# Loops on VectorE and ScalarE, and a semaphore for each pair of engines, in a decode kernel of grouped-query attention beside a Mish block

## The chip, the core and the metric

The kernel runs on one core of a Trainium2 chip. Its engines work side by side: TensorE (matmuls; PE in the profile, and PEld for its weight loads), VectorE (DVE), ScalarE (ACT), GpSimd (POOL) and SyncE (SP), which here issues the big loads. Each has its own stream of instructions and takes them in order; between engines only semaphores order the work. The 16 DMA engines of the core bring data from memory into the on-chip memory, and also the engines' own instructions. The metric is the device time of one launch in microseconds (us), the median of several runs.

## The reference

Eight sequences decode one token each. Two branches read the same `x` (8 rows of 512) and are added to it:

```python
xn = _layernorm(x, axis=-1)
return x + _A_ref(xn, A_k_cache, A_v_cache, A_wq, A_wo) + _B_ref(xn, B_w1, B_b1, B_w2)
```

`_A_ref` is attention with 32 query heads on 8 key/value heads (4 queries each), over a cache of 8192 positions of 128 numbers: `q = xn @ wq`, scores against all keys, softmax, the weighted sum of the values, `@ wo`. `_B_ref` is a dense layer of 1792, the Mish activation `h * tanh(softplus(h))` and a dense layer back to 512. All is float32. The two caches alone are 537 MB, and each of their bytes is used once.

## The kernel before

**Packs.** The work on the caches is cut into 16 packs (`PACKS`). A pack is a pair of key/value heads of two sequences; for each of the two sequences, `b` = 0 and 1, it has 8 MB of keys and 8 MB of values. Pack `p` computes its own scores and weights and, in the same stretch, the output of pack `p - 1`, whose weights are ready. The main loop (line 916 on) does this for each `b`:

- `scores(b, ...)`: 32 matmuls of the pack's queries `qT[:, b]` with 16 blocks of keys, into `C[b]`; ScalarE copies the result to `sc`; `rows(b)` puts it in place in `S`.
- Between the two, on TensorE, the leftovers of the pack before: `sums`, `merge`, and on VectorE `over` (one over the softmax's sums) and `collect`; every fourth pack also `turn`, which brings four packs' outputs into the layout for `wo`.
- After `rows(1)`: `maximum` (VectorE and TensorE by turns), `expand(p + 1)` (VectorE writes the next pack's `qT`, one product for each `b`), `exponents` (ScalarE, then a transpose on VectorE), `fold`, `weights`, `row_sums`.
- `values(b, ...)`: 32 matmuls of the weights `pt` with the values, into `O[b]`; `gather(b)` on VectorE adds up the parts of `O[b]` into `os`.
- In some packs `queries` (a new pair of heads, with `wq`) or `outputs` (with `wo`).

**Loads.** There are three places for streamed data: `kva`, `kvb` and `kvw`. After pack 0 the keys go through `kvb`, which is a quarter larger than one load, so that a load may start when three quarters of the keys before it have been read (the blocks are read forwards and backwards by turns). The values go through `kva`, the projection weights through `kvw`. `plan` (line 357) queues the loads in a fixed order, `pump` and `release` (346 to 355) issue the next one when its place is free. All go out from SyncE in that order, one `dma_start` each, and wait on TensorE's semaphore for the last matmul that reads what they overwrite. So a load that waits holds up the loads behind it.

**The recording layer.** The kernel's calls are recorded by `Program` (line 69), which finds for each operation which earlier ones it must wait for, and `emit` (190) writes the instructions. Each engine counts up one semaphore. TensorE's packs 1 to 15 are one body in a loop on TensorE (`nc.tensor.Fori`, line 253), with tests for the parts that not every pack has. A body that is the same in each pass can't wait for a growing count, so what TensorE waits for is given as tokens (`token="dve"`, `"act"`, `"ev"`) which it takes back by lowering the semaphore (`take`, line 124). In `expand` the token is on the product of `b` = 1 (line 599), and TensorE takes it ahead of `scores` of `b` = 0 (line 923). VectorE, ScalarE, GpSimd and SyncE have all 16 packs written out, one after the other. Where a pack's buffers rotate, `ring` (324) gives two (`os`, `nms`, `l`, `ls`, `r`, `nr`). Line 228 is the one place in `issue` where instructions are made, so nearly all rows of the profile name it.

```python
with nc.tensor.Fori(*LOOP) as pack:
    for name, ops in body:
```

Of the kernel before, what the change touches and what calls it, by code (L numbers as in the profile page):

```python
# [12 lines left out]
P = 128  # L13
# [48 lines left out]
STREAMS = ("k0", "k1", "k", "v", "v0", "va", "vb", "w", "wa", "wb", "w1", "b1", "w2a", "w2b", "w2c")  # L62


ENGINES = ("vector", "scalar", "gpsimd", "sync", "tensor")
LOOP = (1, PACKS)


class Program:
# [4 lines left out]

    def __init__(self, nc):
        self.nc = nc
        self.ops = {e: [] for e in ENGINES}
        self.know = {e: {} for e in ENGINES}
        self.seen = {}
        self.given, self.taken = {}, {}  # L80
        self.signals = set()
        self.pack, self.parts = None, {}
        self.before, self.after = [], []
        self.on_chip, self.psum = set(), set()

    def __getattr__(self, engine):
        if engine not in ENGINES:
            raise AttributeError(engine)
        return Engine(self, engine)

# [6 lines left out]
    def learn(self, engine, op):  # L97
        know = self.know[engine]
        for who, n in (*op.clock.items(), (op.who, op.n)):
            know[who] = max(know.get(who, -1), n)  # L100

    def enter(self, pack):
        self.pack = pack
        if pack is not None:
            self.parts[pack] = []
            self.part(None)

    def part(self, name):

        if self.pack is not None:  # L110
            self.parts[self.pack].append((name, []))

    def keep(self, op):

        if self.pack is None:
            at = self.after if self.parts else self.before
            at.append(op)
            op.place = (self.parts != {}, len(at))
        else:
            parts = self.parts[self.pack]  # L120
            parts[-1][1].append(op)
            op.place = ("loop", len(parts), len(parts[-1][1]))

    def take(self, sem, n=1):

        self.taken[sem] = self.taken.get(sem, 0) + n
        op = Op("tensor", "take", (sem, n), {})
        op.who, op.n, op.waits = "tensor", -1, []
        self.learn("tensor", self.given[sem][self.taken[sem] - 1])
        self.keep(op)  # L130

    def add(self, op, outs, ins, token=None, stream=None):
        engine = op.engine
        op.who = stream or engine
        needs = []
        for ap, writes in [(a, False) for a in ins] + [(a, True) for a in outs]:
            r = self.region(ap)
            seen = self.seen.setdefault(ap.tensor.name, {})
            psum = ap.tensor.name in self.psum
            bank = (r[2] // 512, (r[3] - 1) // 512)  # L140
            for (who, wrote, q), o in seen.items():
                if who == "tensor" == engine:
                    continue
                both = r[0] < q[1] and q[0] < r[1] and r[2] < q[3] and q[2] < r[3]
                hit = both and (writes or wrote)
                if psum and who != engine:
                    hit = bank[0] <= (q[3] - 1) // 512 and q[2] // 512 <= bank[1]
                if hit and self.know[engine].get(who, -1) < o.n:
                    needs.append(o)
        op.waits = []  # L150
        for o in sorted(needs, key=lambda o: -len(o.clock)):
            if self.know[engine].get(o.who, -1) >= o.n:
                continue
            latest = max((x for x in needs if x.who == o.who), key=lambda x: x.n)
            if engine == "tensor" and latest.who in self.given and latest.who in STREAMS:
                self.take(latest.who, latest.n + 1 - self.taken.get(latest.who, 0))
                continue
            assert engine != "tensor" or self.pack is None, (op.method, op.args, latest.who)
            self.wait(op, latest)
        op.token = token  # L160
        if engine == "tensor":
            self.keep(op)
        everyone = self.given.setdefault(stream, []) if stream else self.ops[engine]
        op.n = len(everyone)
        op.clock = dict(self.know[engine])
        everyone.append(op)
        if stream:
            self.ops[engine].append(op)
        if token:
            self.given.setdefault(token, []).append(op)  # L170
        for ap, writes in [(a, False) for a in ins] + [(a, True) for a in outs]:
            self.seen[ap.tensor.name][op.who, writes, self.region(ap)] = op
        return op

    def wait(self, op, other):
        if other.who == "tensor":
            self.signals.add(other.place)
        elif other.token:
            rest = self.ops[other.who][other.n :]
            other = next(o for o in rest if not o.token and o.who == other.who)  # L180
        self.learn(op.engine, other)
        op.waits.append(other)

    def end(self, op):

        last = Op("sync", "done", (), {})
        last.who, last.n, last.waits = "sync", len(self.ops["sync"]), [op]
        self.ops["sync"].append(last)

    def emit(self, tests):  # L190
        nc = self.nc
        sems = {}

        def sem(name):
            if name not in sems:
                sems[name] = nc.alloc_semaphore(f"s_{name}")
            return sems[name]

        count = {}
        for e in ENGINES:  # L200
            n = 0
            for op in self.ops[e]:
                if op.who != e:
                    count[op] = 16 * (op.n + 1)
                elif (op.place in self.signals) if e == "tensor" else not op.token:
                    n += 1
                    count[op] = n

        def issue(op):
            engine = getattr(nc, op.engine)  # L210
            if op.method == "take":
                name, n = op.args
                n *= 16 if name in STREAMS else 1
                engine.wait_ge(sem(name), n).then_inc(sem(name), -n)  # L214
                return
            *first, last = op.waits or [None]
            for w in first:
                engine.wait_ge(sem(w.who), count[w])
            if op.method == "done":
# [9 lines left out]
            if last is not None:  # L229
                got.wait_op(sem(last.who), count[last], "sem-ge")  # L230
# [4 lines left out]
            elif op.engine != "tensor" or op.place in self.signals:  # L235
                got.then_inc(sem(op.engine), 1)
# [802 lines left out]
```

## Time and profile before

| | |
|---|---|
| median of 3 runs | 1309.33 us (1309.3 to 1311.3) |
| the profiled execution | 1311.0 us |
| its span, first to last instruction | 1308.8 us |
| TensorE busy | 881.2 us, 67% of the span |
| VectorE busy | 386.0 us, 592 instructions |
| ScalarE busy | 122.2 us, 294 instructions |
| read from memory | 561.01 MB, 429 GB/s over the span |
| mean granted clock of TensorE | 0.832 |

How to read it. The span is what the profiler saw between the first and the last instruction; the execution's own time is 2.2 us longer. A row of the timeline has the start in us, the duration, the engine, the line, the operation, what it writes and reads, and in brackets how long the engine had been idle before it and what ended that. SPq is SyncE's queue: the row of a load is its issue. The DMA view gives for each kind of load its count and the microseconds from issue to landing; issue plus that number is the landing. Its queue rows give packets, MB and the share of the 16 DMA engines' time in the stretch that was asked for; "instruction" marks an engine's own code. A row of the waits gives who waited for whom: us in total, how often, the longest.

### The profile page before, as it was taken

What the parts mean: (1) busy time and instruction counts of PE and PEld (TensorE: products, weight loads), DVE (VectorE), ACT (ScalarE), POOL (GpSimd) and SP (SyncE); (2) the same over time, 40 slices, a digit from 0 to 9 for tenths busy, and PEclk for the clock granted to TensorE, in tenths of its full rate; (3) what the DMA queues carried; (4) which work ended last, traced back from release to release, by engine and by line L of the source; (5) the groups of instructions that cost most, each with busy time, mean ns of one, the idle gap of its engine ahead of it and who ended that gap; (6) DMA issues with size and microseconds to landing.
All of it is one profiled execution on the core that took longest, in us unless ns stands there. A gap on an engine that the chain in (4) does not pass through costs nothing. (4 is left out here: it accounts for less than half of the span.)

```text
span 1308.8 us, 10954 instructions
## 1 busy us (share of the span) xinstructions
PE 881.2 (67%) x4766; PEld 321.2 (25%) x4766; DVE 386.0 (29%) x592; ACT 122.2 (9%) x294; POOL 4.8 (0%) x10
## 2 busy tenths in 40 slices
PE   5886657856568765686656686665775656766666
PEld 1222222322222222232222222222232222322223
DVE  6250504305051140521405032052320505114051
ACT  1020202001020100201102020020200102001020
POOL 1000000000000000000000000000000000000000
PEclk8887789887888777887877887778887878877779
DMA  9999999999999999999999999999999999999997
GB/s 402 445 415 435 427 447 421 443 425 441 425 443 423 443 423 441 424 443 425 439 431 437 411 449 427 429 439 427 441 427 439 429 437 431 433 429 435 423 434 325
DMA packets 11414, 561.25 MB, mean 429 GB/s; under 512 B 1276, under 2 KB 1408, under 8 KB 1544
## 3 DMA queue, kind: packets, MB, share of 16 engines
q1 hardware_dynamic: 11376, 561.06, 99.4%
q8 instruction: 6, 0.10, 0.0%
q14 instruction: 8, 0.07, 0.0%
q10 hardware_dynamic: 24, 0.02, 0.0%
HBM read 561.01 MB, written 0.07 MB: 429 GB/s over the span
## 5 line engine op out<-in xcount | busy, mean ns | idle before, releaser
L228 PE MATMUL c<-kvb,qT 128*64 128x512 f32 x1984 | 501.1, 669 | 325.9 <-PEq L214 325.9
L228 PEld LDWEIGHTS c<-kvb,qT 128*64 128x64 f32 x1984 | 170.2, 154 | 656.7 <-issue 656.7
L228 PE MATMUL o<-kva,pt 128*32 128x512 f32 x1984 | 249.9, 656 | 23.7 <-PEq L214 23.7
L228 DVE TENSOR_REDUCE nm<-s 128x1 f32<-128x1024 f32 x16 | 19.6, 1225 | 448.4 <-PE s L228 448.4
L228 PEld LDWEIGHTS o<-kva,pt 128*32 128x32 f32 x1984 | 95.6, 119 | 170.2 <-issue 154.8
L228 DVE STREAM_TRANSPOSE raw<-e 128x2048 f32<-128x2048 f32 x36 | 126.3, 3507 | 19.4 <-ACT e L228 18.8
L228 ACT COPY sc<-c 128x512 f32<-128x512 f32 x32 | 18.8, 586 | 981.0 <-PE c L228 981.0
L228 ACT ACTIVATE e<-s,nms 128x512 f32<-128x512 f32 x128 | 88.0, 688 | 133.3 <-DVE nms L228 69.8
L228 DVE RECIPROCAL r<-m 128x16 f32<-128x16 f32 x16 | 4.1, 257 | 234.9 <-PE m L228 234.9
L228 DVE TENSOR_SCALAR os<-o,isel 128x128 f32<-128x128 f32 x32 | 11.2, 351 | 153.4 <-PE o L228 153.4
L228 DVE TENSOR_TENSOR pt<-raw 64x256 f32<-64x256 f32 x128 | 53.6, 418 | 3.6
L228 PE MATMUL s<-sc,csel 64*128 64x512 f32 x128 | 37.9, 664 | 11.0 <-PEq L214 11.0
L228 DVE TENSOR_TENSOR raw<-raw 128x1024 f32<-128x1024 f32 x32 | 39.2, 1225 | 1.1
L228 DVE TENSOR_TENSOR qT<-qc,bsel 128x1024 f32<-128x1024 f32 x32 | 37.7, 1219 | 0.0
L228 DVE SCALAR_TENSOR_TENSOR os<-o,isel,os 128x128 f32<-128x128 f32 x96 | 33.7, 351 | 3.4
L228 ACT ACTIVATION_READ_ACCUMULATOR e<-s,nms 128x1 f32 x128 | 24.7, 193 | 0.0
L228 PE MATMUL m<-ident,nm 128*1 128x128 f32 x16 | 4.4, 276 | 22.6 <-PEq L214 22.6
L228 PE MATMUL h<-kvw,xnT 128*64 128x512 f32 x64 | 17.5, 696 | 0.0
L228 DVE TENSOR_SCALAR e<-h 128x512 f32<-128x512 f32 x16 | 11.1, 691 | 18.3 <-PE h L228 17.9
L228 PE MATMUL m<-hsel,os 128*128 128x8 f32 x66 | 12.5, 262 | 4.7 <-DVE os L228 3.3
L228 PEld LDWEIGHTS m<-hsel,os 128*128 128x128 f32 x66 | 9.9, 190 | 18.8 <-issue 12.2
L228 PEld LDWEIGHTS s<-sc,csel 64*128 64x128 f32 x128 | 10.8, 190 | 14.6 <-issue 14.4
(87 smaller groups left out, 163.0 us busy)
## 6 DMA issues: line engine op xcount, KB each, us to landing
kvw<-in_wq SPq DMA_DIRECT2D x4, 2048.0 KB, 30.5
kvw<-in_wo SPq DMA_DIRECT2D x3, 2048.0 KB, 29.9
kva<-in_v SPq DMA_DIRECT2D x1, 6144.0 KB, 25.0
kva<-in_w SPq DMA_DIRECT2D x1, 3584.0 KB, 15.8
kva<-in_v SPq DMA_DIRECT2D x1, 2048.0 KB, 28.1
kvb<-in_w SPq DMA_DIRECT2D x1, 2048.0 KB, 20.3
kvw<-in_wo SPq DMA_DIRECT2D x2, 1024.0 KB, 24.3
kvb<-in_w SPq DMA_DIRECT2D x1, 1024.0 KB, 24.1
```

What stands on the lines that cost most here:

```text
L228: got = getattr(engine, op.method)(*op.args, **op.kw)
```

## The change

The recording layer is written anew, and the kernel's order of calls is kept but for small shifts. What it does:

1. **Loops on three engines.** TensorE, VectorE and ScalarE each have packs 1 to 15 as one body in a loop of their own, with tests for `turn`, `queries` and `outputs` where the engine has a part in them. VectorE's written-out stream of packs becomes a prologue with pack 0, the body, and an end part; so does ScalarE's. GpSimd and SyncE stay written out.
2. **A semaphore for each pair.** An operation signals at most one engine, on a semaphore named after giver and receiver (`vector_tensor`, `tensor_sync`, ...); parts that are not in every pack have semaphores of their own. `giver` picks the operation whose signal covers a need: the one needed, or the first later one that signals the same receiver. At the end of each pass the receiver lowers its semaphores by what a pass adds. TensorE's `take` instructions inside the body go.
3. **Relays.** Where an operation already signals one engine and a second needs to know, the first receiver passes it on: a wait that signals. The load that overwrites values waits for such a relay on VectorE, placed ahead of `gather`; those of `wq`, `wo` and `w1` go through VectorE too, and the first load of values through ScalarE (ahead of its copy). Loads of keys still wait for TensorE directly.
4. **Register addresses.** `expand` and `collect` differ from pack to pack in where they read or write; in the body the address comes from the loop's register (`vary`).
5. **One buffer for each tile.** `ring` goes; `nms`, `l`, `ls`, `rt`, `nr` are single, `os` is one for each `b`. `collect` moves ahead of `over`, since `rt` is single. Two memsets are added to the prologue (`rt` and 16 columns of `M`), one goes.
6. **Signals of `expand`.** In pack 0 and in the body, the product of `b` = 0 signals TensorE; that of `b` = 1 signals nobody, and is covered by a later signal.
7. **The end.** GpSimd's clearing of the semaphores, beside the output's transfer, goes.

The core of it (left out: the bookkeeping that numbers the signals, and the renaming of tiles):

```diff
-LOOP = (1, PACKS)
+LOOPED = ("tensor", "vector", "scalar")
+FIRST, END = 1, PACKS
...
+    def relay(self, engine, to, after):
+        return self.add(Op(engine, "relay", to=to), [after])
...
-        for e in ENGINES[:-1]:
-            for op in self.ops[e]:
-                issue(op)
-        for op in self.before:
-            issue(op)
-        with nc.tensor.Fori(*LOOP) as pack:
-            for name, ops in body:
...
+        for o in self.ops:
+            if o.place[1] == "before" or o.engine not in LOOPED:
+                issue(o, o.pack)
+        for engine, parts in self.bodies():
+            e = getattr(nc, engine)
+            mine = [c for c in self.low if c[1] == engine]
+            for c, n in (*self.low.items(), *self.early.items()):
+                if c[1] == engine:
+                    lower(engine, c, n)
+            with e.Fori(FIRST, END) as pack:
+                for ops, at in parts:
+                    if name := ops[0].part:
+                        with e.If_eq(e.to_reg(SOMETIMES[name](pack)), 0):
+                            for o in ops:
+                                issue(o, pack)
...
+                for c in mine:
+                    lower(engine, c, self.round[c])
...
-            sp.dma_start(t[:, cols], rows[:, cols], stream=stream)
+            sp.dma_start(t[:, cols], rows[:, cols], stream=stream, to="tensor", after=held.pop(at, ()))
...
-    def expand(p):
-        k = p % NP
+    def expand(later):
         for b in range(PB):
-            dve.tensor_mul(
-                qT[:, b],
-                qc[:, k * PB + b]
...
-                token="dve" if b == PB - 1 else None,
+            dve.vary(
+                "tensor_mul",
+                lambda p, b=b: (
+                    qT[:, b],
+                    qc[:, bass.ds(((p + later) & (NP - 1)) * PB + b, 1)]
...
             if p > 0:
-                values(b, landed.pop(("v", p - 1, b)))
-                gather(p - 1, b)
-                release(("v", p - 1, b))
+                last = values(b, landed.pop(("v", p - 1, b)))
+                read = prog.relay("vector", "sync", last)
+                gather(b)
+                release(("v", p - 1, b), read)
```

More of the change, by code (lines that the diff above doesn't have):

```diff
@@ L132, in add @@
[L132 to L171, printed above, removed]
@@ L613, in scores @@
                 )
-        act.copy(sc, C[b], token="act")
+        read = prog.relay("scalar", "sync", last) if relay else None
+        act.copy(sc, C[b])
+        return read
     def rows(b):
-        prog.take("act")
         for c in range(2):
```

723 lines of the change are left out of this document (413 added, 310 removed).

## Prediction

> **What bounds the kernel now.** I read the page's head and its DMA queues first, then the tail of the timeline, then the loads one by one (the timeline of SyncE gives each issue, the DMA view of a short window its microseconds to landing).
>
> ```profile
> span 1308.8 us, 10954 instructions
> ...
> PE 881.2 (67%) x4766; PEld 321.2 (25%) x4766; DVE 386.0 (29%) x592; ACT 122.2 (9%) x294; POOL 4.8 (0%) x10
> ...
> q1 hardware_dynamic: 11376, 561.06, 99.4%
> q8 instruction: 6, 0.10, 0.0%
> q14 instruction: 8, 0.07, 0.0%
> ```
>
> The queue of SyncE's loads, q1, takes 99.4% of the 16 DMA engines' time. VectorE is busy for 29% and ScalarE for 9%, so the engines that the change rewrites are far from the bound. Two more queues carry instructions: 14 packets in all, a thirtieth of a percent of the bytes. Next the end:
>
> ```profile
> kvb<-in_w SPq DMA_DIRECT2D x1, 512.0 KB, 26.0
> ```
> ```profile
> 1278.92 0.44 SPq L228 DMA_DIRECT2D kvb<-in_w  x1
> ...
> 1305.11 0.62 PE L228 MATMUL h<-kvb,aT 128*8 128x128 f32 x16
> ...
> 1306.11 0.35 SPq L228 DMA_DIRECT2D out<-acc  x1
> ```
>
> The last load, issued at 1278.92, lands 26.0 later, at 1304.9; TensorE multiplies it at once (1305.11), and the result is sent at 1306.11. So the end is the landing of the last load plus 3.9 us. The question for every edit is whether it moves a landing.
>
> What moves landings? Take three loads of 8 MB that follow each other.
>
> ```profile
> 264.25 0.33 SPq L228 DMA_DIRECT2D kva<-in_v  x1
> 288.29 0.33 SPq L228 DMA_DIRECT2D kvb<-in_kT  x1
> 305.11 0.33 SPq L228 DMA_DIRECT2D kva<-in_v  x1
> ```
> ```profile
> kva<-in_v SPq DMA_DIRECT2D x1, 31.3
> ```
> ```profile
> kvb<-in_kT SPq DMA_DIRECT2D x1, 27.3
> ```
> ```profile
> kva<-in_v SPq DMA_DIRECT2D x1, 29.9
> ```
> ```profile
> q14 instruction: 1, 0.01, 1.0%
> ```
>
> They land at 295.6, 315.6 and 335.0: steps of 20.0 and 19.4. The second is the pace of q1 (8 MB at the full rate of the DMA engines), and it comes back below in every step that nothing disturbs. The 20.0 holds the last row, the packet of q14 in the window 311 to 313. The same row answers for 632 to 634, 899 to 901 and 1190 to 1192, and each time the step around it is long. The last of these four:
>
> ```profile
> 1143.00 0.33 SPq L228 DMA_DIRECT2D kva<-in_v  x1
> 1167.93 0.33 SPq L228 DMA_DIRECT2D kvb<-in_kT  x1
> ```
> ```profile
> kva<-in_v SPq DMA_DIRECT2D x1, 31.2
> ```
> ```profile
> kvb<-in_kT SPq DMA_DIRECT2D x1, 26.6
> ```
>
> They land at 1174.2 and 1194.5, a step of 20.3, or 0.9 over. The four excesses are 0.7, 0.9, 1.0 and 0.9 to 1.0, together 3.6 us. Two other packets of q14 (windows 217 to 219 and 775 to 777) cost nothing; for the second:
>
> ```profile
> 742.83 0.33 SPq L228 DMA_DIRECT2D kva<-in_v  x1
> ...
> 765.20 0.33 SPq L228 DMA_DIRECT2D kvb<-in_kT  x1
> ```
> ```profile
> kva<-in_v SPq DMA_DIRECT2D x1, 33.6
> ```
> ```profile
> kvb<-in_kT SPq DMA_DIRECT2D x1, 30.6
> ```
>
> Landings 776.4 and 795.8: 19.4. Whose packets are these? The dear ones come about every 290 us, the cheap ones 558 us apart; VectorE's 592 instructions in 1309 us make 131 in 290 us, ScalarE's 294 make 125 in 558 us. So a packet holds some 128 instructions, the dear four are **VectorE's code**, the cheap two ScalarE's. My reading, which the rows suggest but don't prove: a load has landed when the slowest of its 16 DMA engines is through; VectorE's code always comes through the one that is already last, and what that one loses is never made good, since q1 never empties.
>
> **The change, part by part.**
>
> *Code packets.* VectorE's packs 1 to 15 become one body. The four packets of VectorE in the loop's time go, except perhaps one where the body first runs into its next 128 instructions. Gain: between 0 (another DMA engine is equally late) and 3.6; I take 3.1, nearer the upper end, because the cheap packets show that the other engines lag by at least one packet less. ScalarE's two packets go at no gain. The code must then stay in the engine's store. The trace has one loop already, TensorE's, and these are all packets while it runs (160 to 1270):
>
> ```profile
> q1 hardware_dynamic: 8885, 479.35, 100.0%
> q14 instruction: 6, 0.05, 0.0%
> ```
>
> Not one packet of q8, whose six lie before and after: TensorE's body, the longest, is fetched once and jumped back into without another fetch. [...]
>
> *The first pass's queries.* `scores` of pack 1 waited on a token that the second of `expand`'s two products gives. With a semaphore for each pair, the first product, which alone it reads, gives the signal.
>
> ```profile
> 51.21 0.33 SPq L228 DMA_DIRECT2D kvb<-in_kT  x1
> 71.10 0.33 SPq L228 DMA_DIRECT2D kva<-in_v  x1
> 92.17 0.33 SPq L228 DMA_DIRECT2D kvb<-in_kT  x1
> ```
> ```profile
> kvb<-in_kT SPq DMA_DIRECT2D x1, 25.1
> ```
> ```profile
> kva<-in_v SPq DMA_DIRECT2D x1, 24.6
> ```
> ```profile
> kvb<-in_kT SPq DMA_DIRECT2D x1, 24.4
> ```
> ```profile
> 76.06 2.35 DVE L228 TENSOR_TENSOR qT<-qc,bsel 128x1024 f32<-128x1024 f32 x2
> ...
> 78.71 16.86 PE L228 MATMUL c<-kvb,qT 128*64 128x512 f32 x64 [3.02 <-PEq L214]
> ```
>
> These loads land at 76.3, 95.7 and 116.6: steps of 19.4 and 20.9. The third was issued only 3.5 us before its forerunner landed, the second 5.2 us, and only the third lost time, 1.5 us: between those leads a load comes too late to keep q1 full. Its issue hangs on these scores, which start at 78.71, right behind the two products (76.06, 2.35 long). One product is half of that, so they start 1.2 us sooner and the load is issued at 91.0, a lead of 4.7. Gain: 0 to 1.5; I take 1.2. In later packs the queries are ready long before their keys, so nothing more comes of it.
>
> *V's release through VectorE.* SyncE no longer waits for `values`' last matmul but for a relay on VectorE, ahead of `gather`. Queued behind the relay are `gather` and the second half of the weights; SyncE waits for it with V's next load, and K's load stands behind that.
>
> ```profile
> DVE nm L228 <- PE s L228: 448.4, 16, 30.0
> ...
> DVE os L228 <- PE o L228: 153.4, 32, 12.3
> ```
> ```profile
> kvb<-in_kT SPq DMA_DIRECT2D x31, 26.1
> kva<-in_v SPq DMA_DIRECT2D x30, 31.2
> ```
>
> In all 32 gathers VectorE already stood waiting for TensorE's `o`, so the relay passes the signal on without queueing. The trace has no relay; it costs at least nothing and at most what VectorE is late. A V load is issued 31.2 − 19.4 = 11.8 us before its forerunner lands; against the 5.2 that sufficed above, 6.6 us may be lost before it shows. Price 0; without that cover, the excess in each of 30 loads. K's loads (lead 6.7) still hang on TensorE directly. The load at 71.10 now goes through ScalarE, whose next work is the copy of the same scores, so it waits there anyway: 0.
>
> *Loops and register addresses.* VectorE gets a branch back, three tests, address arithmetic for two products in `expand` and one in `collect`, and lowerings of semaphores; ScalarE gets a branch back and lowerings. No row shows them on these engines. Below: 0. Above: VectorE's wait ahead of `nm`, 448.4 us in 16, is 28 us a pack that the additions may fill. TensorE loses its decrements inside the body for some at its end, while it waits for K. I take 0 for all. `collect` ahead of `over` and the single buffers follow VectorE's own order, and their readers were done a pack earlier: 0. The prologue's two other memsets and the relay that frees `w1` come while VectorE waits: 0.
>
> **Sum.** 3.1 + 1.2 = 4.3 us. The profiled execution took 1311.0 us, 2.2 around its span; it would become 1306.7, with a span of 1304.5. The runs' median, 1309.33, lies 1.7 below that execution, so the forecast is **1305.0**. With both gains at their ends (5.1, or 2.7 with the first at 1.5), 1304.2 to 1306.6. A measurement of this kernel can tell about 0.2%, or 2.6 us, from no change.
>
> **Rivals.**
> 1. *The code is fetched again in each pass* (slower). Place: the jump back, 14 times. Price: 0.9 us for each packet on VectorE's DMA engine. More than five packets (4.3 / 0.9) eat the gain. With one a pass, 14 × 0.9 = 12.6 us: 1317.6; with two, 1330. Against it: TensorE's loop fetches nothing. For it: TensorE's store need not be like VectorE's. [...] Chance 0.12.
> 2. *Another DMA engine is just as late* (no change to be seen). The long steps then stem from VectorE's packets, but the second slowest engine follows within a few tenths, and only the earlier issue in pack 1 counts: 1309.33 − 1.2 = 1308.1. For it: TensorE's six packets fall on some DMA engines too. Against it: four jumps in a row by one kind of packet, none by the other. Chance 0.13.
> 3. *The relay comes too late.* If VectorE's additions cost over 6.6 us between `nm` and the relay, 30 loads of V lose what is over; at 1 us over, 1335. Against it: ten instructions can hardly take that. Chance 0.02.
>
> **How the numbers follow.** The forecast has 0.73, and its own range is 1303.6 to 1306.6 (the bounds above, and 0.6 below, since three runs from 1309.3 to 1311.3 fix their median no better). Rival 1 and 3 lie far off with 0.14; to hold 0.8 the range must reach over rival 2, to 1309. Faster by over 0.2% is below 1306.7: 0.73. Within: 0.13. Slower: 0.14.
>
> **What would show it.** In the profile after: about two packets of q14 between 160 and 1270 where there are six; no 8 MB step above 19.5 in the loop; scores of pack 1 at about 77.5 and K's next load at about 91.0; 3.9 us from the last landing to the end, as now. Rival 1 shows as dozens of packets on q14, rival 2 as a last landing about 1.2 us sooner with the packets gone, rival 3 as V loads landing in under 25 us. The forecast is wrong if landings do not follow the packets at all.

## The result, and the profile after

The changed kernel takes 1307.17 us (median of 22 executions, 1306.07 to 1310.88), the kernel before beside it 1309.86 (1308.97 to 1311.55, 22 executions). The ratio after to before is 0.9983, with a 95% interval of 0.9976 to 0.999: faster by 0.17%, a little under the 0.2% at which the prediction begins to count a gain; the interval leaves no change out. Forecast were 1305.0 and a range of 1303.6 to 1309.0. Ten of the 22 executions lie between 1306.07 and 1306.52, the others trail off above. The execution that was profiled is one of those above: 1310.0 us, span 1307.9. So the profile is read by stretches, and not by its end alone.

The page of the changed kernel, its head, its engines and its queues:

```profile
span 1307.9 us, 11284 instructions
...
PE 876.0 (67%) x4766; PEld 272.8 (21%) x4766; DVE 389.9 (30%) x596; ACT 122.2 (9%) x294; POOL 4.8 (0%) x10
...
q1 hardware_dynamic: 11376, 561.06, 99.4%
q8 instruction: 7, 0.11, 0.0%
...
q14 instruction: 3, 0.02, 0.0%
```

The bound is the same: q1 at 99.4%. The queue of VectorE's and ScalarE's code, q14, has 3 packets in the span and not 8. All three lie outside the loop (80 bytes at 0.2, 8 KB each at 39.7 and 1285.6), for these are all the queues in the DMA view of the changed kernel for the loop's time, 160 to 1270:

```profile
## 3 DMA queue, kind: packets, MB, share of 16 engines
q1 hardware_dynamic: 8915, 480.94, 100.2%
```

Where the prediction shows q14 with 6 packets, there is no row of it. Next the same three loads as the prediction's, from the timeline of SyncE (start of the issue, length) and the DMA view of the issue's window (microseconds to landing):

```profile
264.87 0.33 SPq L386 DMA_DIRECT2D kva<-in_v  x1
289.03 0.33 SPq L386 DMA_DIRECT2D kvb<-in_kT  x1
305.62 0.33 SPq L386 DMA_DIRECT2D kva<-in_v  x1
```
```profile
kva<-in_v SPq DMA_DIRECT2D x1, 31.5
```
```profile
kvb<-in_kT SPq DMA_DIRECT2D x1, 26.6
```
```profile
kva<-in_v SPq DMA_DIRECT2D x1, 29.4
```

They land at 296.4, 315.6 and 335.0: steps of 19.2 and 19.4, where the first was 20.0 before. By the landings in hundredths (the moment at which the last of a load's 16 DMA engines signals its end, from the trace) every 8 MB step in the loop is 19.34 to 19.36.

That part came as forecast. The start did not. In the timeline of the changed kernel, from the prologue to pack 1:

```profile
24.29 1.68 PE L386 MATMUL h<-acc,gsel 4*8 4x448 f32 x8 [6.21 <-DVEq L383]
...
34.62 0.33 SPq L386 DMA_DIRECT2D kva<-in_kT  x1
...
73.86 0.33 SPq L386 DMA_DIRECT2D kva<-in_v  x1
...
78.52 2.35 DVE L386 TENSOR_TENSOR qT<-qc,bsel 128x1024 f32<-128x1024 f32 x2
...
79.88 16.67 PE L386 MATMUL c<-kvb,qT 128*64 128x512 f32 x64 [1.74 <-DVE qT L386]
...
93.15 0.33 SPq L386 DMA_DIRECT2D kvb<-in_kT  x1
```

The rows of `mish` and of K (0,1) in the kernel before:

```profile
20.03 1.68 PE L228 MATMUL h<-acc,gsel 4*8 4x448 f32 x8 [2.97 <-DVE e L228]
...
30.33 0.33 SPq L228 DMA_DIRECT2D kva<-in_kT  x1
```

`mish` starts on TensorE at 24.29 and not at 20.03, after 6.21 us of waiting for VectorE's queue where it waited 2.97; `w1` is free, and K (0,1) issued, at 34.62 (30.33 before). Scores of pack 1 do start 1.36 us after the start of the first of the two products, as the prediction says, but the products come later. And at the end:

```profile
1284.68 9.84 PE L386 MATMUL o<-kva,pt 128*32 128x512 f32 x64 [1.31 <-DMA kva<-in_v]
...
1302.95 1.05 PE L386 MATMUL h<-kvw,oW 128*8 128x128 f32 x32
1303.83 0.61 PE L386 MATMUL h<-kvb,aT 128*8 128x128 f32 x16
1304.83 0.35 SPq L386 DMA_DIRECT2D out<-acc  x1
```

The last load lands at 1303.07; TensorE is still on the part before it, and the last part starts at 1303.83, 0.76 after the landing. The stretches of the two profiled executions, by landings:

```
                                        before   after    difference
K (0,1): step                            19.35   20.42    +1.07
V (0,0): step                            19.35   20.45    +1.10
K (1,1): step                            20.83   19.34    -1.49
all that to landing 155                                   +0.75
155 to 1270, the loop                  1116.75  1112.99   -3.76
the last V load (6 MB): step             14.56   15.67    +1.11
last landing                           1304.97  1303.07   -1.90
last landing to the end of the span       3.8      4.8     +1.0
```

The loop gives 3.8 us; the start and the end give most of it back in this execution. Which of these belong to the change, and which to this one execution, the experiments have to say. A step is long in two ways in these two profiles, and the 16 signals of a load tell them apart. When the load was issued too late, the first signal is late too (V (0,0) of the changed kernel: 0.63 us, K (0,1): 0.93). When a code packet held up one DMA engine, one signal moves and the other 15 stay (in the kernel before, around the packet at 632: the last one goes from 3.34 to 4.28 us after the first, the next to last stays at 2.61).

### The profile page after: what moved, and what is told of

The parts are those of the page before. It is cut to its first block, busy times and chain, and to the rows that moved or that the text cites. A ratio compares the mean times of both kernels' runs of the same rounds, so it can differ in the third digit from the quotient of the medians.

```text
span 1307.9 us, 11284 instructions
## 1 busy us (share of the span) xinstructions
PE 876.0 (67%) x4766; PEld 272.8 (21%) x4766; DVE 389.9 (30%) x596; ACT 122.2 (9%) x294; POOL 4.8 (0%) x10
## 2 busy tenths in 40 slices
DMA packets 11410, 561.21 MB, mean 429 GB/s; under 512 B 1277, under 2 KB 1409, under 8 KB 1545
## 3 DMA queue, kind: packets, MB, share of 16 engines
q1 hardware_dynamic: 11376, 561.06, 99.4%
## 4 chain that ended last, share of the span: by engine, by line
DMA 63%; PE 34%; DVE 2%; ACT 0%; issue 0%; POOL 0%; DVEq 0%; ACTq 0%; SPq 0%
DMA kvb<-in_kT 60%; PE c L386 31%; DMA kva<-in_v 2%; DMA kva<-in_kT 2%; PE h L386 2%; PE o L386 1%; DVE raw L386 0%; PE m L386 0%; ACT wide L386 0%; DVE wide L386 0%; DVE nm L386 0%; DVE st L386 0%; PE s L386 0%; POOL pt L386 0%; DMA sc<-in_x 0%
## 5 line engine op out<-in xcount | busy, mean ns | idle before, releaser
L386 PEld LDWEIGHTS c<-kvb,qT 128*64 128x64 f32 x1984 | 154.2, 155 | 670.3 <-DMA kvb<-in_kT 349.7
L386 PE MATMUL o<-kva,pt 128*32 128x512 f32 x1984 | 244.3, 649 | 25.4 <-DMA kva<-in_v 24.8
L386 DVE STREAM_TRANSPOSE raw<-wide 128x2048 f32<-128x2048 f32 x36 | 125.3, 3482 | 15.9 <-ACT wide L386 14.0
L386 PEld LDWEIGHTS o<-kva,pt 128*32 128x32 f32 x1984 | 65.7, 118 | 193.9 <-issue 152.2
L386 ACT ACTIVATE wide<-s,nms 128x512 f32<-128x512 f32 x128 | 88.0, 687 | 129.6 <-DVE nms L386 66.2
L386 DVE TENSOR_TENSOR oT<-m,rt 128x16 f32 (+1 forms) x17 | 3.0, 175 | 231.6 <-PE m L386 231.6
L386 ACT ACTIVATION_READ_ACCUMULATOR wide<-s,nms 128x1 f32 x128 | 24.7, 193 | 0.0
L386 PE MATMUL c<-kva,qT 128*64 128x512 f32 x64 | 15.6, 649 | 3.0 <-DMA kva<-in_kT 3.0
L386 DVE TENSOR_SCALAR wide<-h 128x512 f32<-128x512 f32 x16 | 11.1, 691 | 19.6 <-PE h L386 19.2
```

The costliest lines, as they stand in the source:

```text
L386: got = getattr(engine, o.method)(*args, **kw)
```

## The experiments

Main theory: an 8 KB packet of code holds up one of the 16 DMA engines, and costs time if that is the one which ends every load; VectorE's packets did, and the loop takes them away. Rivals: the long steps went for another reason (semaphores, relays); any code packet costs; the second gain, the earlier scores of pack 1, is real or not.

All times are of one chip for each group of runs; "loop" is the stretch between the landings at about 155 and 1270, which hold the same loads in each kernel.

**VectorE written out, ScalarE written out, the settling wait, the changed kernel again.** The first two edits:

```diff
-LOOPED = ("tensor", "vector", "scalar")
+LOOPED = ("tensor", "scalar")          # e1_vector_out
+LOOPED = ("tensor", "vector")          # e2_scalar_out
```

> The changed kernel with VectorE's packs 1 to 15 written out again; ScalarE keeps its loop, and the semaphores for each pair of engines, the register-free queries, the relays and the buffers stay. Theory A (VectorE's code packets lengthen landings): four packets of q14 come back inside 160 to 1270, each in an 8 MB step of 20.0 to 20.4 where the others take 19.35, 3.5 to 3.8 us in all; the time is 3 to 4 us above the changed kernel's on the same chip, about 1310. Theory B (the long steps went for another reason, the pairs' semaphores or the relays): the steps stay at 19.35 and the time stays within 1 us of the changed kernel's.

> The changed kernel with ScalarE's packs 1 to 15 written out again; VectorE keeps its loop. Theory A (only packets on the DMA engine that is already last cost time, and ScalarE's go through others): one or two packets of q14 come back inside 160 to 1270, no 8 MB step in the loop is above 19.45, and the time stays within 0.6 us of the changed kernel's. Rival (each code packet costs a step, whoever's it is): 0.9 us for each packet, 0.9 to 1.8 us more.

The third moves one wait in `queries`:

```diff
             )
+        prog.settle("vector")
         dve.transpose(qt, qs)
...
-        prog.settle("vector")
         return read
```

> The changed kernel with the settling wait in queries put ahead of the transpose, right behind the four scale copies that read h, so that TensorE's next product on h need not wait for the transpose and the copy of the queries. Theory A (the late product delays the load that takes w1's place, which then comes too late to keep q1 full): mish's first matmul at 21 to 21.5 and not 24.3, the load of K (0,1) issued at about 31.5, its step 19.4 and not 20.4, the time 1.0 to 2.2 us below the changed kernel's (2.2 if the step of V (0,0), 20.45, goes with it). Rival (the load's step of 20.4 has another cause, or the queue makes it good later): no difference over 0.3 us.

> The changed kernel once more, on the same chip as the three above, as their base, and for a second profile. Expected: 1306 to 1307.5, no packet of q14 between 160 and 1270, every 8 MB step in the loop 19.34 to 19.36. If the late end of TensorE in the changed kernel's profile belongs to the program, values of the last pack again end 1 us or more later against the landing than before (9.8 against 8.5); if it belongs to that execution alone, they don't.

```
                    median   range               ratio to before, 95%       loop
before (31 runs)    1309.62  1308.59 to 1311.72
e1_vector_out       1309.63  1309.26 to 1312.47  1.0004, 0.9995 to 1.0013   1116.52
e2_scalar_out       1307.13  1306.06 to 1312.12  0.9990, 0.9979 to 1.0002   1113.04
e3_early_settle     1306.20  1306.04 to 1307.88  0.9974, 0.9963 to 0.9985   1113.02
e4_changed_again    1306.38  1306.12 to 1311.88  0.9982, 0.9972 to 0.9991   1113.25
```

With VectorE written out the whole gain is gone. Its q14 row of the window 160 to 1270, then the loads on both sides of one of the four packets (window 576 to 579), issue and microseconds to landing:

```profile
q14 instruction: 4, 0.03, 0.0%
```
```profile
q14 instruction: 1, 0.01, 0.7%
```
```profile
540.68 0.33 SPq L386 DMA_DIRECT2D kva<-in_v  x1
563.52 0.33 SPq L386 DMA_DIRECT2D kvb<-in_kT  x1
```
```profile
kva<-in_v SPq DMA_DIRECT2D x1, 34.6
```
```profile
kvb<-in_kT SPq DMA_DIRECT2D x1, 32.1
```

Landings 575.3 and 595.6, a step of 20.3: the packets are back, at other places in the program, and the long steps stand with them. The four are 0.22, 0.97, 0.96 and 0.96 over, and 0.4 more stands in two steps without a packet; the loop is 3.5 longer than in the changed kernel's third profile below (1113.02). The semaphores, relays and buffers of the change are all still in this kernel, so the rival is out.

With ScalarE written out two packets come back:

```profile
q14 instruction: 2, 0.02, 0.0%
```

and the loop is as short as without them, 1113.04. They are not on the DMA engine that ends the loads. The trace lets one see it: of the 16 signals at a load's end, in order, the one that a packet of ScalarE hit came 0.2 us after the first, then 0.9, after the second packet 1.5, while the last came 2.0 after the first all the time. That the moved signal belongs to the DMA engine of the packet is read from the times; the trace doesn't name the engine. The median of this kernel, 0.75 above the changed kernel's, comes from its upper executions (five of 11 are at the low end, 1306.06 to 1306.27), and its interval can't tell them apart.

With the settling wait ahead of the transpose, `mish` starts at 21.34 and K (0,1) is issued at 31.56; its step is 19.36. This is the timeline of e3_early_settle:

```profile
21.34 1.68 PE L386 MATMUL h<-acc,gsel 4*8 4x448 f32 x8 [3.24 <-DVEq L383]
...
31.56 0.33 SPq L386 DMA_DIRECT2D kva<-in_kT  x1
```

So the late wait is the change's own cost at that place. But the median moves by 0.2 us and not by 1 to 2.2. The changed kernel's second profile has the late issue too (34.35, a step of 21.15), and the step of V (0,0) is 19.46 there: the two had not the same cause. Of the 1.8 us that K (0,1) loses in that second profile, 0.5 stand in the load's first signal, which is the late issue; by the rest the last falls further behind the first. So the late issue is not the whole of it. What remains open here, why the median hardly follows, is taken up below under the spread.

**The earlier scores by themselves, before again, and twice the code.**

```diff
-                token="dve" if b == PB - 1 else None,
+                token="dve" if b == 0 else None,          # e5_first_token, in the kernel before
```
```diff
                 row_sums()
+                for i in range(37):                       # e7_out_double, e8_loop_double
+                    dve.memset(idle[:, i : i + 1], 0.0)
```

> The kernel before with one word changed: of expand's two products the first, not the second, tells TensorE. Nothing else of the change is in it. Theory A (the prediction's second gain is real in most executions): scores of pack 1 start 1.2 us sooner, the step of K (1,1) is about 19.4 and not 20.8, and the time is 1.2 to 1.5 us below the kernel before. Theory B (the 1.5 us of the profile of before belong to that one execution, in which TensorE's first scores were slow; in most executions K (1,1) is issued early enough anyway): the time is within 0.4 us of the kernel before.

> The kernel before once more, for a second profile. Theory B of the run above: if this execution takes about 1309.5, the step of K (1,1) is below 20 and the lead of its issue 4.5 us or more; the four long steps in the loop are there again and add up to 3.4 to 3.8. Theory A: the step is 20.5 or more again.

> VectorE written out as in the first run, with 37 more instructions on VectorE at the end of each pack (memsets of single elements of a tile that nothing reads), so that its stream is about twice as long; they take 2 to 3 us of the 28 us for which VectorE waits in each pack. Theory A (each of VectorE's code packets costs a saturated load queue up to 0.95 us): about 8 packets of q14 between 160 and 1270 and not 4, and the time 3 to 4 us above the first run's, about 1313. Rival (the long steps are not the packets' doing, or the second slowest DMA engine soon sets the pace): no more than 1 us above it, about 1310.

> The changed kernel with the same 37 memsets in VectorE's loop. Theory A: no packet of q14 between 160 and 1270, every step in the loop 19.34 to 19.36, the time within 0.4 us of the changed kernel's, about 1306.4. Rival (the work itself delays loads): the time rises as in the run above.

```
                    median   range               ratio to before, 95%       loop
before (21 runs)    1309.54  1308.83 to 1311.93
e5_first_token      1309.58  1308.96 to 1311.16  0.9999, 0.9990 to 1.0008   1116.26
e6_before_again     1308.70  one execution                                  1115.88
e7_out_double       1316.70  1315.84 to 1316.95  1.0054, 1.0041 to 1.0068   1123.99
e8_loop_double      1306.25  1306.14 to 1310.38  0.9985, 0.9976 to 0.9994   1112.99
```

The earlier signal alone shows no gain; the interval reaches from 1.3 us faster to 1.0 slower, so the median alone can't shut out the forecast 1.2. Its mechanism is there: in e5_first_token the scores of pack 1 start at 77.42, as forecast.

```profile
75.90 2.35 DVE L228 TENSOR_TENSOR qT<-qc,bsel 128x1024 f32<-128x1024 f32 x2
...
77.42 15.45 PE L228 MATMUL c<-kvb,qT 128*64 128x512 f32 x64 [1.89 <-PEq L214]
```

There was little to be had, and this the profiles show. In the second profile of the kernel before, K (1,1) is issued 4.6 us ahead of its forerunner's landing, and its step is 19.54 and not 20.83. In the first profile, on which the prediction rested, the issue was 3.5 ahead; and of the 1.5 us only the half is the late issue: the first of the load's 16 DMA engines is 0.75 late, the last falls back by a further 0.74, and a code packet of TensorE (q8, at 101.8) lies in that step. In e5_first_token the load goes out 6.2 ahead, its first signal is on time, and yet the step is 19.75 and not the expected 19.4: the last signal alone is 0.4 late, again with a packet of TensorE in the step (101.5).

The second profile of before also misses what was expected of its loop: three steps are long and not four (0.90, 0.97 and 1.01 over, 2.9 together). VectorE's first packet, at 312.4, moves one signal from 1.2 to 2.2 us after the first, just short of the last, and costs nothing. In e5_first_token it costs 0.10, in e1_vector_out 0.22, in the first profile of before 0.69.

Doubling VectorE's code costs nothing in a loop, and 7.1 us written out (1316.70 against 1309.63). The window 160 to 1270 of e7_out_double has 8 packets, as expected:

```profile
q14 instruction: 8, 0.07, 0.0%
```

Seven of them stand in steps of 20.32 to 20.41, the one at 160 in 19.59; one more, at 1277 and outside the window, stands in 20.38. That is 0.97 to 1.06 each, 8.3 us with the small one, and more than the 3 to 4 us that I expected, which counted the packets of the first run at their mean. A further 2.7 us stand in steps with no packet (20.19 and 20.18 the longest), all after the last DMA engine had fallen 4.8 us behind the first. A late issue is not the reason for these two: the loads went out over 10 us ahead, 15 signals kept their pace, and only the last one moved (from 4.6 to 5.5 and from 4.8 to 5.6 after the first). The cause stays open.

The looped twin is the clearest evidence for the first step: the same 37 memsets in each pack, 592 in all, one packet of q14 at 152.8, the next at 1282, and 1306.25.

**ScalarE's code made longer.** The theory says more than "VectorE's packets cost". It says that a packet of anyone costs as soon as its DMA engine is the last. In e2_scalar_out, with a longer stream:

```diff
                 row_sums()
+                for i in range(37):
+                    act.copy(idle[:, i : i + 1], ones[:1, :1])
```

> The changed kernel with ScalarE written out and with 37 more instructions on ScalarE at the end of each pack (copies of one element to a tile that nothing reads), so that its stream is about three times as long; VectorE keeps its loop. Six or seven packets of q14 should come between 160 and 1270. In the run with ScalarE written out its two packets each put their DMA engine 0.6 to 0.7 us further behind (from 0.2 to 0.9 to 1.5), while the last engine stood at 2.0. Theory A (a packet costs nothing until its DMA engine is the last one, and then all of it): the first two or three long steps fail to appear, the rest take 0.3 to 1.0 over 19.35 each, 2 to 3.6 us in all, the time about 1308.3 to 1310. Rival 1 (only VectorE's packets cost): no step above 19.45, about 1306.3. Rival 2 (each packet costs a step at once): 5.7 us or more, about 1312.

The median is 1310.55 (1308.93 to 1312.15, 10 executions), the ratio to before 1.0003 (0.9994 to 1.0013), and the loop takes 1116.05. The profile, window 160 to 1270:

```profile
q14 instruction: 6, 0.05, 0.0%
```

The packets come at 298, 463, 631, 854, 1017 and 1187. For each, the step that it stands in, and how long after the first of the 16 DMA engines the last one signals:

```
packet at   298     463     631     854    1017    1187
step        19.34   19.61   20.04   20.04   20.02   20.03
last after  1.88    2.10    2.78    3.44    4.13    4.81
```

The first is free (so was one at 91, ahead of the window), the second costs 0.26, and then each costs 0.67 to 0.69: 3.0 us together, within the 2 to 3.6 expected (the median is 0.5 above the expected times, which left the spread out). Both rivals (no cost, or 5.7 us at once) are out. One row more to see it in: the loads around the packet at 631.

```profile
584.28 0.33 SPq L386 DMA_DIRECT2D kva<-in_v  x1
```
```profile
kva<-in_v SPq DMA_DIRECT2D x1, 29.8
```
```profile
607.76 0.33 SPq L386 DMA_DIRECT2D kvb<-in_kT  x1
```
```profile
kvb<-in_kT SPq DMA_DIRECT2D x1, 26.3
```

Landings 614.1 and 634.1: a step of 20.0 from a packet of ScalarE, in a kernel in which VectorE's loop stands as in the changed one.

**The spread.** The settling wait and the changed kernel once more, on one chip:

> The kernel of the third run (settling wait ahead of the transpose) once more, for its spread beside that of the changed kernel on the same chip. Theory A (the late load of K (0,1) is what sends some of the changed kernel's executions to 1308 to 1312): at most one execution in ten is above 1308 where the changed kernel has about one in three or four, and the medians are within 0.5 us. Rival (the late executions have other causes): as many above 1308 as in the changed kernel.

> The changed kernel a third time, beside the run above: a median of 1306.2 to 1307.2, about one execution in three or four above 1308. In its profile the step of K (0,1) is above 19.5 if its load is issued less than 4 us ahead of its forerunner's landing, and 19.4 if more.

```
                    median   range               ratio to before, 95%       loop
before (25 runs)    1309.96  1308.75 to 1311.50
e10_settle_again    1306.30  1306.20 to 1309.35  0.9974, 0.9965 to 0.9984   1113.07
e11_changed_third   1307.62  1306.17 to 1310.69  0.9984, 0.9975 to 0.9993   1113.02
```

Above 1308 are 2 of the 16 executions with the early settling wait, and 17 of the 45 of the changed kernel in its three sets. That points the way of the theory, but chance would give as large a gap about one time in nine: it isn't settled. In e10_settle_again alone 2 of 9 are above, where at most one in ten was expected, and the median of e11_changed_third is above the expected 1306.2 to 1307.2. A second cause shows in the profiles. Windows of two stretches, 56 to 74 (scores of K (0,1)) and 1270 to 1303 (the end); the third number from the right is TensorE's granted clock. First the changed kernel's profile of 1310.0 us, then e11_changed_third, whose profiled execution took 1306.17, then e10_settle_again, 1309.35:

```profile
56.00:74.00 18.00, 15.57 (x64) 4.80 (x64) 0.00 (x0) 0.08 (x1) 0.00 (x0) 0.91 1.02 441
1270.00:1303.00 33.00, 27.97 (x284) 11.51 (x288) 4.45 (x15) 0.41 (x2) 0.00 (x0) 0.74 0.90 380
```
```profile
56.00:74.00 18.00, 15.08 (x68) 4.81 (x68) 0.96 (x1) 0.58 (x1) 0.00 (x0) 1.00 0.96 416
1270.00:1303.00 33.00, 25.43 (x322) 10.54 (x314) 3.87 (x13) 0.41 (x2) 0.00 (x0) 0.88 0.87 364
```
```profile
56.00:74.00 18.00, 16.34 (x68) 5.21 (x68) 0.00 (x0) 0.58 (x1) 0.00 (x0) 0.91 0.96 416
1270.00:1303.00 33.00, 28.09 (x303) 11.94 (x306) 4.79 (x17) 0.41 (x2) 0.00 (x0) 0.75 0.89 377
```

V (0,0) overwrites K (0,1), so it waits for these scores. At a clock of 0.91 in the first stretch it is issued 15.7 and 15.8 us after K (0,1) has landed, only 3.6 us ahead of its forerunner's landing, and its step is 20.45 and 20.79; at 1.00, here and in the profiles of before (both), e1 to e5 and e8_loop_double, it is issued after 14.1 us, the lead is 5.2 us or more and the step 19.34 to 19.46. At a clock of 0.74 to 0.79 in the second stretch (these two and e3_early_settle) the result is sent 1.65 to 1.76 us after the last landing, at 0.85 and above 1.05 to 1.14. So two of the losses of the changed kernel's profile (V (0,0), the late end) go with where the low spells of the clock fell in that execution. The third profile of the changed kernel has neither, and no loss at K (0,1) (lead 4.5, step 19.35).

A third cause is TensorE's own code. The last V load of the changed kernel's profile, 1.11 too long, was issued 10 us ahead, and of its 16 signals one moves to 3.43 us behind the first, where the last had been 2.29 behind, while the others keep their pace; a packet of 16 KB of TensorE (q8, at 1277.2) lies in the step. K (1,1) of e10_settle_again was issued 6.5 us ahead and takes 20.89: the last signal goes from 2.35 to 3.89, the other 15 stay, and the packet is at 101.6. This is what e9_scalar_long showed of ScalarE's packets (up to 0.69 us each), in a third engine's code, read from two executions; in most others the same packets cost 0.4 us at most. How much of the spread each of the three causes makes is not shown.

**How long may the loop's body be?** The prediction's first rival, made to happen:

```diff
                 row_sums()
+                for i in range(560):
+                    dve.memset(idle[32 * (i % 4) : 32 * (i % 4) + 1, i // 4 : i // 4 + 1], 0.0)
```

> The changed kernel with 560 memsets of single elements (of a tile that nothing reads) at the end of each pack in VectorE's loop, so that its body has 635 instructions and not 75; at the 14 ns a memset of the run with 37 they take some 8 us of the 17 us for which VectorE waits there. Theory A (a looped body is fetched once, however long, as TensorE's is): no packet of q14 after the first pass but those of ScalarE's and VectorE's ends, every step 19.34 to 19.36, the time within 0.6 us of the changed kernel's, 1306.2 to 1307. Rival (the prediction's first rival: the engine's store holds fewer instructions than that, and the body is fetched again in each pass): 635 by 128, or 5 packets a pass, 70 and more in all, each worth up to 0.95 us: up to 1370. [...]

1709.31 us (1706.59 to 1711.98, 4 executions; ratio 1.3037, 1.3014 to 1.3061). The code is fetched again in each pass, as the rival has it. The time is far above the rival's price, and most of it has another reason. The page of this kernel, then its q14 row for the window 160 to 1600:

```profile
span 1710.0 us, 20244 instructions
...
q1 hardware_dynamic: 11376, 561.06, 76.7%
q14 instruction: 109, 0.89, 0.1%
```
```profile
q14 instruction: 98, 0.80, 0.2%
```

98 packets in some 14 passes are seven a pass. q1 falls from 99.4% to 76.7%: the queue now runs empty, and why is in the timeline. One pass, first VectorE, then TensorE:

```profile
499.76 53.12 DVE L386 MEMSET idle<- 1x1 f32 x560
555.95 0.17 DVE L386 TENSOR_TENSOR oT<-m,rt 128x16 f32 x1 [3.07 <-issue]
```
```profile
557.09 1.97 PE L386 MATMUL m<-oT,wide 128*128 128x64 f32 x8 [40.43 <-DVE wide L386]
```

The memsets, expected to take 8 us, last 53.1, and not because VectorE waits for code. They take 53.10 to 53.15 in all 16 packs, pack 0 included, which stands ahead of the loop; from a pack's third on, each starts 91 to 100 ns after the one before, with no gap where a packet comes. The 14 ns of the expectation are those of e8_loop_double:

```profile
471.83 0.51 DVE L386 MEMSET idle<- 1x1 f32 x37
```

There the memsets write one row of the tile, here four rows by turns; whether this makes them slower, no run here shows. What the fetch costs VectorE stands at the jump back: the next instruction starts 2.8 to 3.1 us after the branch (0.19 in the changed kernel, 0.29 in e8_loop_double), and two of the pass's packets are fetched right behind the branch (552.8; 553.8 and 556.3). Over 14 jumps that makes some 37 us, an estimate from these waits, of the 402 by which this kernel is longer than the changed one. The rest goes, as far as the rows tell, with the memsets: behind them TensorE waits 40 us for VectorE, and V's load for TensorE. It goes out at 569.1, 23 us after its forerunner landed (546.0). SyncE's wait for VectorE's relays, here and in the changed kernel:

```profile
SPq L386 <- DVEq L383: 1243.0, 32, 62.8
```
```profile
SPq L386 <- DVEq L383: 522.1, 32, 32.3
```

So two bodies, of 75 (changed kernel) and 112 instructions (e8_loop_double), have no packet of q14 between 160 and 1270, and the body of 635 has some seven a pass (98 between 160 and 1600), with 2.8 to 3.1 us of waiting at the jump back. At which length between 112 and 635 the fetching in every pass begins, no run here shows.

## Why the prediction was right, and where not

The median, 1307.17, lies in the range, 1303.6 to 1309.0, and the main step was right. That the number fits is in part luck. The range of the forecast itself ended at 1306.6 and was stretched to 1309 for the second rival, which did not come. And the ratio, 0.9983, is a gain of less than 0.2%, an outcome to which the prediction gave 0.13.

- **Code packets** (forecast 3.1, bounds 0 to 3.6): right in mechanism and size. The loop is 3.8 shorter between the first two profiles, 2.9 between e6_before_again and e11_changed_third, and 3.5 comes back with VectorE written out. The step "VectorE's code always comes through the one that is already last" says too much: in the second profile of before the first packet only makes its DMA engine nearly the last (0 us), and then each costs 0.9 to 1.0. What the runs show is that a packet pushed back its own DMA engine, and cost only what set this one behind the one that was last until then (ScalarE's longer stream, e9_scalar_long: 0 us for the first packet, 0.26 for the second, then 0.67 to 0.69 each). "ScalarE's two packets go at no gain" held as well (1113.04 against 1113.02). The forecast of about two packets left in the loop was high by two; there are none.
- **The first pass's queries** (forecast 1.2, bounds 0 to 1.5): this is the term that failed; no gain shows (ratio 0.9999, 0.9990 to 1.0008, that edit alone). The prediction took a loss of 1.5 us from one execution for a property of the program, and put all of it down to the late issue, which made half. Scores do start 1.3 us sooner (77.42 against 78.71); but the second profile of before has 0.2 us to lose there. Without this term the forecast would have been 1306.2, where the low cluster of the changed kernel lies (1306.07 to 1306.52).
- **The relay that frees `w1`** (put at 0, because it comes "while VectorE waits"): wrong at its place; what it costs the median is open. The forecast looked at the relay, and not at what TensorE waits for ahead of it: `mish`'s first product waits on VectorE's settling after the transpose and the copy of the queries, 3 us that it did not wait before. With the wait moved, `w1`'s load comes 3 us sooner and its step is 19.36 and 19.35; with it in place, the step was 20.42 and 21.15 in two profiles, where the lead was 3.1 and 3.6, and 19.35 in the third (lead 4.5). In e1_vector_out, e2_scalar_out and e7_out_double to e9_scalar_long, where it is in place too, the step is 19.19 to 19.37. So it can be one reason for the 1.0 us by which the median lies above the low cluster; the runs don't settle it.
- **V's release through VectorE** and **loops and register addresses** (0 each): right. Every 8 MB step in the loop is 19.34 to 19.36, and 37 more instructions a pack don't change it. With 53 us more work a pass on VectorE, V's loads do come too late (e12_loop_long).
- **"3.9 us from the last landing to the end"**: 4.8 in the profile of after, 4.1 in the third (1299.95 to 1304.08). Of the 1.0 us more, 0.6 stand ahead of the issue of the result and go with the clock in the last 33 us. The other 0.4 stand behind it in all three profiles of the changed kernel (3.07 to 3.08, before 2.68 to 2.69), where ScalarE's last instructions come later; with ScalarE written out it is 2.81.
- **The rivals.** Code fetched in each pass: did not happen with this body, happens with a long one, and shows there as a wait of 2.8 to 3.1 us at each jump back. The prediction's one or two packets a pass were assumed, and no run shows them; the long body took some seven. The price of 0.9 us a packet could not be seen, since q1 ran empty (76.7%). Another engine just as late: out, the loop is 2.9 to 3.8 shorter. The relay too late: out with this body.

No kernel here is shown to beat the changed one. The one with the early settling wait has the lowest ratio, 0.9974 in both sets (0.9963 to 0.9985, 0.9965 to 0.9984), and its interval overlaps with the changed kernel's (0.9972 to 0.9991, 0.9975 to 0.9993).

## What to carry to other kernels

In this kernel, whose load queue kept the DMA engines 99.4% busy, straight-line code was not free: with VectorE's written out the loop took 3.5 us longer (e1_vector_out, 1116.52 against 1113.02), with twice that code 11.0 (e7_out_double, 1123.99). Where a load queue is as full, count the instruction packets by queue, look which of them stand in long steps, and loop that engine's code, with a body well below the length at which it is fetched again (112 instructions were not, 635 were). A stall seen in one profiled execution is worth something only if a second profile shows it; take it into a forecast at the size that both share. When a wait is moved to another engine's signal, look at what that engine does before it gives the signal. And time a filler instruction in the form in which it will stand: a memset took 14 ns in one edit (37 in 0.51 us, e8_loop_double) and 95 in the next (560 in 53.1 us, e12_loop_long).

## What was not expected of the hardware

- A packet of 8 KB takes 0.31 to 0.33 us itself in most cases, but holds its DMA engine up by 0.90 to 1.06 us (VectorE's, once it is the last) or 0.67 to 0.69 us (ScalarE's); one of TensorE's, 16 KB and 0.96 us long, by 1.5 us (e10_settle_again). Why longer than the packet itself is not shown. VectorE's code and ScalarE's each kept to one DMA engine, to judge by the signals at the loads' ends: in the kernel before, VectorE's packets at 632 and 899 each moved the last signal alone (from 3.34 to 4.28 and from 3.22 to 4.20 us after the first), and in e9_scalar_long ScalarE's last four each moved it on by 0.66 to 0.69.
- What the last DMA engine loses was not made good in the loop: in e9_scalar_long its lag behind the first grew by steps from 1.9 to 4.8 us and shrank in none between.
- A jump back into a body that is fetched again (e12_loop_long) keeps VectorE waiting 2.8 to 3.1 us, against 0.19 us in the changed kernel.
- In these profiles seven loads of 8 MB were issued 3.1 to 3.64 us ahead of their forerunner's landing. All had their first signal 0.5 to 1.0 us late, and six had steps 1.1 to 2.2 us too long (one of them, K (1,1) in before, with half of it from elsewhere); the seventh, at 3.64, lost nothing. Two at 3.75 and 3.77 took 19.36 and 19.37. How far apart the forerunner's signals lie seems to count too, by one load: in e1_vector_out, with 4.7 us between its first and last, a load issued 5.7 us ahead of the last had its first signal 0.96 late.
